# A two-problem cached decode attention on one core: q for two groups into four PSUM banks, wo as 512 + 64 columns of one weight load, and the output blocks folded on GpSimd before they are gathered

## Chip, core and metric

One core of one Trainium2 chip. The metric is device microseconds of one launch; a kernel's time is the median of its runs. A core has five engines that run their own instruction streams: TensorE (PE, with its weight loads PEld), VectorE (DVE), ScalarE (ACT), GpSimd (POOL) and SyncE (SP, which here only issues DMAs). Sixteen DMA engines move the data from HBM.

## What is computed

Two independent decode steps A and B with the same shapes; their outputs are laid side by side. The reference, cut to one of them:

```python
B, Sq, D = 2, 1, 576
Hq, Hkv, Sk, Dh = 32, 16, 16384, 128
W = min(4096, max(256, Sk // 4))        # 4096
rep = Hq // Hkv                         # 2
q = (x @ wq).reshape(B, Sq, Hq, Dh).transpose(0, 2, 1, 3)
k = jnp.repeat(k_cache[:, :, Sk - W:, :], rep, axis=1)
v = jnp.repeat(v_cache[:, :, Sk - W:, :], rep, axis=1)
scores = jnp.einsum("bhqd,bhkd->bhqk", q, k) * (Dh ** -0.5)
p = _softmax(scores, axis=-1)
o = jnp.einsum("bhqk,bhkd->bhqd", p, v)
return o.transpose(0, 2, 1, 3).reshape(B, Sq, Hq * Dh) @ wo
```

One query token per batch row, 32 query heads on 16 key heads, a window of the last 4096 keys, all in bfloat16. Nearly all bytes are the K and V windows: 2 problems x 2 batches x 16 heads x 4096 x 128 elements for each.

## The kernel before

**Steps and slabs.** The work is cut into 16 steps (ND = 16), eight for A and eight for B. Step s takes the keys of key heads s and s + 8 of both batch rows: one K slab and one V slab of 4 MB each (a partition row of 32 KB). Two steps make a group G = s // 2 (NG = 8); four groups make a problem. Slabs go through a ring of four buffers (`ring`, NR = 4). SP issues the loads in the order of `stream`: wq of A, wq of B, then K and V alternately, V one step behind K; at the end the order is K13, V12, K14, K15, V13, V14, V15. A slab's load waits until the last reader of the slab four places earlier is done (`issue_slab`, L228). V15 is loaded in two pieces of 3 MB and 1 MB with a semaphore each. The rows of wo that a group needs (`wob`, 1.15 MB) are loaded between slabs; those of the last group come at the very end, as one load of 576 KB and three small ones for its last four heads (L281, L266).

**The front.** x of both problems is loaded first and transposed; `do_qproj` (L394) makes q for one group in two PSUM banks (`tb0`, `tb1`), five matmuls of 512 columns each, ACT copies both to `qrow`, DVE transposes (`qtr`), ACT rearranges (`qk`). `init_mask` (L375) makes the mask tile `maskB` with four matmuls and one ACT copy.

**A step.** DVE transposes the K slab in four quarters (`do_X`, L459, buffers `xt`), PE multiplies each quarter with the spread q (`do_S`, eight matmuls of 512 columns over L482 and L166) into the scores bank pair `st0` or `st1`. One step later DVE takes the maximum, PE and DVE turn it into a bias (`do_nm`, `do_nm2`, `do_exp`), ACT does the exponential with its row sums (L527), DVE transposes the result (`do_pC`, L535), POOL spreads the row sums (`do_sum`, L543: `rsel`), PE sums them over the partitions once per group (`do_tot`, L547), and PE multiplies with the V slab (`do_PV`, L574): 32 matmuls of 512 columns, of which four run side by side in four strips of 32 columns of the array, into the bank `acc`. So PV of step c runs at the end of step c + 1 of the loop.

**A group's end.** `acc` holds, in each strip, four blocks of 128 columns of which one is wanted per row. ACT copies it to `acc_sb` (L586); `do_comb` gathers the wanted blocks with four small matmuls per step against `ident_r` (L603) into the bank `ot`, which DVE has set to zero; DVE multiplies with the reciprocal row sums and spreads the result (`do_norm`, L619, L630); `do_redist` turns it with two small matmuls (L661) and ACT copies it (`Rsb`, L669). `do_proj` (L676) then multiplies with wo: for each of eight heads of a batch row two matmuls of 288 columns, with a weight load each, that write to two different strips (partitions 0 and 32 of `ot`):

```python
return OT[32 * half:32 * half + Bb, ACC0:ACC0 + NH]
...
for half in range(2):
    last = e.matmul(proj_out(half), l_, wob[:, pc, s_, half * NH:(half + 1) * NH],
```

**The end.** Every engine's order is the order in which the program adds its instructions; nothing is reordered later. After the loop of steps the order is written out by hand: PV of step 13 in parts between the steps of the last softmax, `tot7`, comb13, norm13, redist6, proj13, PV14, comb14, norm14, the first piece of PV15, redist7, the second piece, comb15, norm15, proj14, proj15, and two copies (`do_E`, one on DVE and one on ACT) and the output DMAs. "PV13" in this text is the V part of step 13, "comb13" its gathering, and so on.

Of the kernel before, what the change touches and what calls it, by code (L numbers as in the profile page):

```python
# [59 lines left out]
def build_kernel(nc, probs, out, cfg=None):  # L60
# [32 lines left out]
    ACC0 = 128  # L93
    assert NOUT % 2 == 0 and ACC0 + NH <= 512
# [11 lines left out]
    with es:  # L106
# [32 lines left out]
        mrow = sb("mrow", [4, 128], BF16)  # L139
        mcol = sb("mcol", [4, 512], BF16)  # L140
# [3 lines left out]
        acc_sb = sb("acc_sb", [128, 512], BF16)  # L144
        ident_r = sb("ident_r", [128, 32], BF16)
        out_sb = sb("out_sb", [34, NPROB, NH], BF16)
# [33 lines left out]
        def load_x(P, eng):  # L180
# [7 lines left out]
        p_zxT = S.add("pool", lambda e: e.memset(xT[:].rearrange("c h p w -> c (h p w)").bitcast(FP32), 0.0), [], "zero_xT")  # L188
        p_zq = S.add("pool", lambda e: e.memset(zq[:].rearrange("d p z w -> d (p z w)").bitcast(FP32), 0.0), [], "zero_zq")
        p_ones_f = S.add("pool", lambda e: e.memset(ones_f[:], 1.0), [], "ones_f")  # L190
        p_ident_f = S.add("pool", lambda e: e.affine_select(ident_f[:], ones_f[:], [[-1, 128]], ALU.is_equal, 0.0,
                                                           base=0, channel_multiplier=1), [p_ones_f], "ident_f")
        p_zc = S.add("pool", lambda e: e.memset(mcol[:], 0.0), [], "zero_mcol")
        p_mcol = S.add("pool", lambda e: e.affine_select(
            mcol[:].rearrange("k (j c) -> k j c", c=4), mcol[:].rearrange("k (j c) -> k j c", c=4),
            [[0, 128], [1, 4]], ALU.is_equal, BIG, base=0, channel_multiplier=-1), [p_zc], "mcol")
        p_mrow = S.add("pool", lambda e: e.affine_select(
            mrow[:].rearrange("k (x c r) -> k x c r", c=4, r=2), ones_b[0:4, :].rearrange("k (x c r) -> k x c r", c=4, r=2),
            [[0, 16], [1, 4], [0, 2]], ALU.is_equal, 0.0, base=0, channel_multiplier=-1), [p_ones_b], "mrow")
# [95 lines left out]
        comb_bank = []  # L295
        q_first = [None, None]
        tb_consumer = {}
# [9 lines left out]
        ot_zero = {}  # L307
        ot_da = {}
        ot_pe = {0: None}
        acc_zero = {}  # L310
# [7 lines left out]
        def tb_job(fn, tag, deps):  # L318
            n = tbn[0]
            tbn[0] += 1  # L320
            bank = TB[n % NTB]
            d = list(deps)
            if n >= NTB:
                d.append(tb_consumer[n - NTB])
            return n, bank, S.add("pe", lambda e: fn(e, bank), d, tag)

        def init_small():
            ot_zero[0] = S.add("dve", lambda e: e.memset(OT[:], 0.0), [], "zero_OT")
            ot_da[0] = ot_zero[0]
            acc_zero[0] = ot_zero[0]  # L330
# [9 lines left out]
                mask4S[:], ident_b[:].rearrange("d (a s) -> d s a", s=4), AX.X, ALU.max), [p_ident_b], "mask4S")  # L340
            init["ident_r"] = S.add("dve", lambda e: e.tensor_reduce(
# [33 lines left out]
        def init_mask():  # L375
            def f(e):
                last = None
                for n_ in range(4):
                    bank = ST[1 - n_ // 2][:, 512 * (n_ % 2):512 * (n_ % 2) + 512]
                    if n_ == 0:  # L380
                        first = last = e.matmul(bank, mrow[:, :], mcol[:, :], start=True, stop=True)
                    else:
                        last = matmul_again(e, first, bank, mcol[:, :], True, True)
                return last
            op = S.add("pe", f, [p_mcol, p_mrow], "maskp")
            init["maskB"] = S.add("act", lambda e: e.activation(maskB[:], ST[1][:, 0:512], ACTF.Copy), [op], "maskB")
            chain[(0, "fill")] = chain[(1, "fill")] = init["maskB"]

        def do_fill(s):
            chain[(s, "fill")] = S.add("act", lambda e: e.activation(  # L390
                ST[s % 2][:, :].rearrange("k (h j) -> k h j", h=2), maskB[:].unsqueeze(1).broadcast_to([128, 2, 512]), ACTF.Copy),
                [init["maskB"], chain[(s - 2, "exp")], chain[(s - 2, "max")], zqev[s]], "fill%d" % s)

        def do_qproj(G):  # L394
            P = G // GPP
            nq = pos[("Q", P)]
            issue_until(nq)
            evs = []
            for nb in range(2):
                hf = nb  # L400
                c0 = nb * HH + 512 * (G % GPP)

                def fn(e, bank, c0=c0, hf=hf, nb=nb):
                    last = None
                    chs = list(range(NFC - 1)) + [NFC, NFC - 1]
                    for k_, ch in enumerate(chs if nb == 0 else chs[::-1]):
                        w_ = ring[:, nq % NR, ch * HD + c0:ch * HD + c0 + 512] if ch < NFC else wqr[:, P, c0 - hf * HH:c0 - hf * HH + 512]
                        x_ = xT[:, ch if ch < NFC else NFC + hf, P, :]
                        if k_ == 0 and q_first[0] == (P, ch):
                            last = matmul_again(e, q_first[1], bank[:, 0:512], w_, True, False, False)  # L410
                        else:
                            last = q_first[1] = e.matmul(bank[:, 0:512], x_, w_, start=(k_ == 0), stop=(k_ == NFC))  # L412
                        q_first[0] = (P, ch)
# [479 lines left out]
```

## Time and profile before

| what | value |
|---|---|
| median of 3 runs | 364.8 us (364.79 to 364.89) |
| the profiled execution: its time | 364.83 us |
| the profiled execution: its span, first to last instruction | 363.2 us |
| DMA | 153.27 MB in 7075 packets, mean 422 GB/s over the span |
| PE, PEld, DVE, ACT, POOL busy | 61%, 18%, 55%, 19%, 5% of the span |
| mean granted PE clock | 0.836 |
| PE instructions in the profile | 1370 matmuls, 1097 weight loads |

The span is what the engines did; some 1.6 us of the execution's time lie outside it. In the page, a row reads: source line, engine, operation, what it writes and reads, shapes, count, then busy time and mean duration of one, then the idle time before it and what ended that. PEclk is the clock that the throttle granted to PE (1.00 or 0.50 over a stretch), DMA share the mean busy share of the sixteen DMA engines.

### The profile page before, as it was taken

The numbers are of one execution on the slowest core, as the hardware profiler recorded it, in microseconds if no ns is written. First come the engines' busy times: TensorE is split into PE (matmuls) and PEld (weight loads), VectorE is DVE, ScalarE is ACT, GpSimd is POOL, SyncE is SP. The second block draws the span as 40 slices with busy tenths as digits, with TensorE's granted clock in tenths as the row PEclk, the third lists the DMA queues.
The fourth block names the chain that finished last, engine by engine and source line by source line (L and its number), as shares of the span: only waits on it lengthen the run. The fifth ranks groups of instructions, "written<-read, shape, count | busy, mean of one in ns | idle before, by whom it ended". The sixth has DMA issues, their size and how long they took to land.

```text
span 363.2 us, 2960 instructions
## 1 busy us (share of the span) xinstructions
PE 220.4 (61%) x1370; PEld 64.6 (18%) x1097; DVE 198.7 (55%) x173; ACT 67.8 (19%) x155; POOL 16.4 (5%) x45
## 2 busy tenths in 40 slices
PE   0399688292836748093754839184673918377875
PEld 0033112020211212021211202021120202111131
DVE  2022796573908476382916658191935649099821
ACT  1046203020300303020300303020020203002121
POOL 5000000000000000000000000000000000000000
PEclk9999899698895969678895958879696978858988
DMA  8999999999999999999999999999999999999994
GB/s 347 433 433 433 433 402 463 415 451 413 423 444 419 444 417 437 437 420 444 416 441 429 433 433 422 431 429 437 407 446 437 426 437 437 420 433 426 431 412 187
DMA packets 7075, 153.27 MB, mean 422 GB/s; under 512 B 780, under 2 KB 1304, under 8 KB 1688
## 3 DMA queue, kind: packets, MB, share of 16 engines
q1 hardware_dynamic: 7056, 153.10, 98.4%
q8 instruction: 9, 0.15, 0.2%
q10 hardware_dynamic: 8, 0.00, 0.0%
q14 instruction: 2, 0.02, 0.0%
HBM read 153.10 MB, written 0.00 MB: 422 GB/s over the span
## 4 chain that ended last, share of the span: by engine, by line
DMA 70%; DVE 14%; PE 12%; ACT 2%; issue 0%; SPq 0%; DVEq 0%
DMA ring<-in_B_k_cache_dram 34%; DMA ring<-in_A_k_cache_dram 25%; DVE xt L459 13%; DMA ring<-in_B_v_cache_dram 8%; PE st L482 4%; PE st L166 4%; DMA x_sb<-in_B_x_dram 3%; PE tb L412 3%; ACT qrow L421 1%; PE tb L166 1%; DVE qtr L427 1%; DVE nM L505 1%; ACT qk L435 0%; PE ot L689 0%; PE tb L495 0%
## 5 line engine op out<-in xcount | busy, mean ns | idle before, releaser
L459 DVE STREAM_TRANSPOSE xt<-ring 128x2048 f32<-128x2048 f32 x64 | 144.9, 2285 | 107.6 <-DMA ring<-in_B_k_cache_dram 59.5
L482 PE MATMUL st<-xt,zq 128*128 128x512 bf16 x256 | 114.6, 448 | 119.9 <-DVE xt L459 119.9
L166 PE MATMUL st<-xt,zq 128*128 128x512 bf16 x256 | 113.0, 441 | 0.0
L482 PEld LDWEIGHTS st<-xt,zq 128*128 128x128 bf16 x256 | 27.5, 107 | 209.2 <-DVE xt L459 136.5
L510 ACT ACTIVATE nMrep<-nM 1x128 f32<-1x128 f32 x16 | 4.9, 308 | 176.8 <-DVE nM L505 176.8
L574 PE MATMUL acc<-ring,pC 128*32 128x512 bf16 x512 | 32.8, 391 | 1.3 <-DMA ring<-in_B_v_cache_dram 1.2
L535 DVE STREAM_TRANSPOSE pC<-pR 128x1024 bf16<-128x1024 bf16 x16 | 19.4, 1214 | 4.3 <-ACT pR L527 2.1
L586 ACT ACTIVATE acc_sb<-acc 128x512 bf16<-128x512 f32 x16 | 9.5, 597 | 63.2 <-PE acc L574 63.2
L492 DVE TENSOR_REDUCE m<-st 128x1 f32<-128x1024 f32 x16 | 19.0, 1190 | 1.0 <-PE st L166 0.9
L527 ACT ACTIVATE pR<-st,bias_sb 128x1024 bf16<-128x1024 f32 x16 | 17.8, 1114 | 0.5
L412 PE MATMUL tb<-ring,xT 128*128 128x512 bf16 x50 | 16.7, 424 | 0.1
L427 DVE STREAM_TRANSPOSE qtr<-qrow 128x512 f32<-128x512 f32 x8 | 5.7, 711 | 19.4 <-ACT qrow L421 19.4
L574 PEld LDWEIGHTS acc<-ring,pC 128*32 128x32 bf16 x512 | 13.1, 98 | 17.1 <-issue 6.0
L543 POOL TENSOR_SCALAR rsel<-maskS,rsum 128x8 f32<-128x8 bf16 x16 | 4.9, 308 | 243.8 <-ACT pR L527 243.8
L390 ACT ACTIVATE st<-maskB 128x1024 f32<-128x1024 bf16 x14 | 14.4, 1028 | 0.4
L446 POOL TENSOR_TENSOR zq<-qk,maskA 128x128 bf16<-128x128 bf16 x16 | 6.4, 400 | 86.7 <-PE st L166 69.6
L421 ACT ACTIVATE qrow<-tb 128x512 bf16<-128x512 f32 x16 | 9.3, 586 | 3.8 <-PE tb L412 3.6
L689 PE MATMUL ot<-wob,Rsb 128*2 128x288 bf16 x120 | 9.5, 303 | 0.3 <-ACT Rsb L669 0.3
L353 PE MATMUL tb<-ident_b,x_sb 4*128 4x4 bf16 x4 | 0.3, 172 | 14.6 <-DVE x_dup L360 14.6
L412 PEld LDWEIGHTS tb<-ring,xT 128*128 128x128 bf16 x50 | 5.2, 106 | 11.7 <-issue 7.8
L412 PE MATMUL tb<-wqr,xT 128*128 128x512 bf16 x16 | 6.7, 417 | 0.0
L505 DVE TENSOR_REDUCE nM<-tb 1x8 f32<-1x128 f32 x16 | 4.4, 273 | 4.1 <-PE tb L495 4.1
(64 smaller groups left out, 79.0 us busy)
## 6 DMA issues: line engine op xcount, KB each, us to landing
ring<-in_A_k_cache_dram SPq DMA_DIRECT2D x8, 4096.0 KB, 30.6
ring<-in_A_v_cache_dram SPq DMA_DIRECT2D x8, 4096.0 KB, 35.4
ring<-in_B_k_cache_dram SPq DMA_DIRECT2D x8, 4096.0 KB, 30.7
ring<-in_B_v_cache_dram SPq DMA_DIRECT2D x7, 4096.0 KB, 35.2
wob<-in_A_wo_dram SPq DMA_DIRECT2D x4, 1152.0 KB, 37.1
ring<-in_A_wq_dram SPq DMA_DIRECT2D x1, 4096.0 KB, 12.7
ring<-in_B_wq_dram SPq DMA_DIRECT2D x1, 4096.0 KB, 21.7
wob<-in_B_wo_dram SPq DMA_DIRECT2D x3, 1152.0 KB, 37.4
```

Of the source, the lines that this page charges most:

```text
L166: return e.add_instruction(mybir.InstMatmult(name=nc.get_next_instruction_name(), engine=i.engine, ins=[e.lower_ap(rhs), i.ins[1]], outs=[ ...
L390: chain[(s, "fill")] = S.add("act", lambda e: e.activation(ST[s % 2][:, :].rearrange("k (h j) -> k h j", h=2), maskB[:].unsqueeze(1).broad ...
L412: last = q_first[1] = e.matmul(bank[:, 0:512], x_, w_, start=(k_ == 0), stop=(k_ == NFC))
L421: evs.append(S.add("act", lambda e, bank=bank, nb=nb: e.activation(qrow[:, 512 * nb:512 * nb + 512], bank[:, 0:512], ACTF.Copy), d, "qrow% ...
L459: Xop[(s, u)] = S.add("dve", lambda e: e.transpose(xt[:, i % NKT, :].rearrange("k (j w) -> k j w", w=64), ring[:, n % NR, :].bitcast(FP32) ...
L482: first = last = e.matmul(bank, zq[:, p4, s % NZQ, w0:w0 + 128], mv, start=False, stop=stop, skip_group_check=True)
L492: chain[(s, "max")] = S.add("dve", lambda e: e.tensor_reduce(m1[:, 0:1], ST[s % 2][:, :], AX.X, ALU.max), d, "max%d" % s)
L527: chain[(s, "exp")] = S.add("act", lambda e: e.activation(pR[:, :], ST[s % 2][:, :], ACTF.Exp, bias=bias_sb[:, 0:1], scale=SCALE, accum_ou ...
L535: chain[(s, "pC")] = S.add("dve", lambda e: e.transpose(pC[:, s % NPT, :, :].rearrange("k j c -> k (j c)"), pR[:, :]), d, "pC%d" % s)
L574: last = e.matmul(ACC[32 * cb:32 * cb + 32, 0:512], pC[:, D_ % NPT, j0_:j0_ + 4, :].rearrange("k j c -> k (j c)"), ring[:, n % NR, j0_ * 1 ...
L586: acc_ev[D_] = S.add("act", lambda e: e.activation(acc_sb[:], ACC[:, :], ACTF.Copy), d, "accev%d" % D_)
L689: last = e.matmul(proj_out(half), l_, wob[:, pc, s_, half * NH:(half + 1) * NH], start=False, stop=True, skip_group_check=True)
```

## The change

PE's instruction list gets 46 matmuls, 143 weight loads and 9 waits shorter, 198 in all:

- **q:** `do_qpair` makes q for two groups at once, in four banks, and runs the four banks one after the other on each loaded x. The 80 matmuls stay; 66 weight loads become 22. `qrow` copies go with it (1024 columns at once for every second pair).
- **mask:** `maskB` is made by two DVE instructions instead of four matmuls and an ACT copy. Three memsets go from POOL to DVE, three POOL instructions go away.
- **fold:** after the ACT copy of `acc`, POOL multiplies with a 0/1 mask and adds the four blocks in two halvings (`accm`, `acca`, `accr`; both steps of a group in one instruction each, in group 6 each step by itself), and `do_comb` needs one small matmul per step. Groups 0 to 6 do so; steps 14 and 15 are gathered as before. `ot` needs no zeroing any more.
- **wo:** for groups 0 to 6 each head is one weight load with a matmul of 512 columns and one of 64 columns. The 512 columns add up in `ot` over a problem's groups, the 64 columns go to a `tb` bank and DVE adds them up in `o_rest`. Before the last two steps, `fin_ops` puts both into the two-strip form, and proj14 and proj15 add to it as before.
- **row sums:** one `rsel` per group (POOL, now a tensor-tensor) instead of two, added to POOL's list in `do_tot`.
- **order in a step:** the last quarter of the scores, `do_S(s, 3)`, waits for pC of the step before (not in the last step); a group's proj comes after it; comb, norm and redist move one quarter later.
- **order at the end:** PV14 comes before comb13; comb13, comb14, redist6 and proj13 come between PV14 and the first piece of PV15. On POOL, the three folding instructions of step 13 stand ahead of `rsel7`.
- **output:** three output DMAs instead of four.

```diff
-        p_zxT = S.add("pool", lambda e: e.memset(xT[:]...
+        p_zxT = S.add("dve", lambda e: e.memset(xT[:]...
...
+        def do_qpair(i):
+            Gs = (2 * i, 2 * i + 1)
...
+            order = [NFC, NFC + 1] + list(range(NFC))
+            if Gs[0] % GPP:
+                order = order[::-1]
+            todo_ = [(ch, b) for ch in order for b in mine(ch)]
...
+                        if q_first[0] == (P, ch):
+                            last = matmul_again(e, q_first[1], banks[b], w_, start, stop, False)
...
         def do_S(s, u):
...
+            if u == NU - 1 and 1 <= s < ND - 1:
+                deps.append(chain[(s - 1, "pC")])
...
-        def do_sum(s):
...
         def do_tot(G):
+            d = [chain[(2 * G, "exp")], chain[(2 * G + 1, "exp")], init["maskS"]]
+            if G >= 1:
+                d.append(chain[(G - 1, "tot")])
+            chain[(G, "rsel")] = S.add("pool", lambda e: e.tensor_tensor(
+                rsel[:, :, :], maskS[:].unsqueeze(1).broadcast_to([128, 2, 8]),
+                rsum[:].unsqueeze(2).broadcast_to([128, 2, 8]), ALU.mult), d, "rsel%d" % G)
...
         def do_PV(D_, rounds, wait):
...
+                acc_ev[D_] = S.add("act", lambda e: e.activation(acc_sb[:, D_ % 2, :], ACC[:, :], ACTF.Copy), d, "accev%d" % D_)
+                G = D_ // 2
+                if not by_group(G) or (D_ % 2 == 0 and G < NG - 2):
+                    return
+                l0, l1 = (0, 2) if G < NG - 2 else (D_ % 2, D_ % 2 + 1)
...
+                t = S.add("pool", lambda e: e.tensor_tensor(
+                    v, v, maskJ[:].unsqueeze(1).unsqueeze(3).broadcast_to([128, l1 - l0, 4, 128]), ALU.mult),
+                    [acc_ev[2 * G + l] for l in range(l0, l1)] + [init["maskJ"]], "accm%d" % D_)
+                t = S.add("pool", lambda e: e.tensor_tensor(a_[:, :, 0:256], a_[:, :, 0:256], a_[:, :, 256:512], ALU.add),
+                          [t], "acca%d" % D_)
...
+                t = S.add("pool", lambda e: e.tensor_tensor(
+                    acc_r[:, l0:l1, :], a_[:, :, 0:128], a_[:, :, 128:256], ALU.add), d, "accr%d" % D_)
...
         def do_comb(D_):
...
+                    for l_ in range(2):
+                        last = e.matmul(bank[:, 8 * l_:8 * l_ + 8], acc_r[:, l_, :], maskS[:, :], start=True, stop=True)
...
         def do_proj(D_):
...
+                        if by_group(G):
+                            first = e.matmul(OT[0:Bb, 0:NB0], l_, wob[:, pc, s_, 0:NB0], start=start and begin, stop=end, skip_group_check=True)
+                            last = matmul_again(e, first, rest[0:Bb, 0:NB1], wob[:, pc, s_, NB0:NOUT], rstart and begin, rstop and end)
...
+                    elif G == NG - 2:
+                        d = [proj[D_], chain[(ND - 2, "exp")], chain[(ND - 2, "max")]]
+                        a_ = S.add("act", lambda e: e.activation(fin(0), OT[0:Bb, 0:NH], ACTF.Copy), d, "fin0")
+                        tb_consumer[n] = S.add("dve", lambda e: e.tensor_tensor(
+                            fin(1)[:, NB0 - NH:NH], o_rest[:, :], bank[0:Bb, 0:NB1], ALU.add), d + [rest_add[G - 1]], "fin1")
+                        fin_ops.append(S.add("dve", lambda e: e.tensor_copy(fin(1)[:, 0:NB0 - NH], OT[0:Bb, NH:NB0]), [a_], "fin2"))
...
         do_PV(D_, range(4, NRD), None)
-        do_sum(s)
         do_tot(s // 2)
+        do_rsb(s // 2)
+        do_PV(ND - 2, range(NRD), None)
         do_comb(D_)
         do_norm(D_)
-        do_rsb(s // 2)
+        do_comb(ND - 2)
         do_redist(D_ // 2)
+        do_norm(ND - 2)
         do_proj(D_)
-        do_PV(ND - 2, range(NRD), None)
-        do_comb(ND - 2)
-        do_norm(ND - 2)
         D_ = ND - 1
```

## Prediction

> **What bounds the kernel now.** First the slices and queues of the page, then the DMA issues.
>
> ```profile
> DMA  8999999999999999999999999999999999999994
> ...
> q8 instruction: 9, 0.15, 0.2%
> ...
> ring<-in_A_k_cache_dram SPq DMA_DIRECT2D x8, 4096.0 KB, 30.6
> ...
> ring<-in_B_v_cache_dram SPq DMA_DIRECT2D x7, 4096.0 KB, 35.2
> ```
>
> The DMA engines never rest between the first slice and the last. A 4 MB slab (4.19 million bytes) takes 9.7 us at the 433 GB/s of most slices; a K slab lands 30.6 us after its issue, a V slab 35.2, so each issue has 21 and 25 us of other transfers ahead of it. Work that delays an issue by less costs nothing. What counts is the end of the stream and what follows the last pieces of V and wo. So next the timeline of the end (start, duration):
>
> ```profile
> 347.48 0.31 POOL L543 TENSOR_SCALAR rsel<-maskS,rsum 128x8 f32<-128x8 bf16 x1 [7.02 <-ACT pR L527]
> 347.85 0.40 PE L547 MATMUL tb<-rsel,ones_f 128*128 128x16 f32 x2 [0.92 <-POOL rsel L543]
> ...
> 350.79 0.61 PE L574 MATMUL acc<-ring,pC 128*32 128x512 bf16 x2
> ...
> 355.61 1.48 PE L574 MATMUL acc<-ring,pC 128*32 128x512 bf16 x24 [0.29 <-DMA ring<-in_B_v_cache_dram]
> ...
> 358.10 0.62 PE L574 MATMUL acc<-ring,pC 128*32 128x512 bf16 x8 [0.88 <-DMA ring<-in_B_v_cache_dram]
> ...
> 359.60 0.66 PE L689 MATMUL ot<-wob,Rsb 128*2 128x288 bf16 x8
> ...
> 360.30 1.12 PE L689 MATMUL ot<-wob,oTn 128*2 128x288 bf16 x8
> ```
>
> PV15's pieces start as they land (355.6, 358.1); proj15 ends on the last rows of wo, whose load ends its chain at 360.95. The two copies end at 361.91; a span of 363.2 and a time of 364.83 follow, 0.03 above the median of 364.8. I sum against 361.91.
>
> Last, PE's clock in stretches of 3.41 us, cut where it changes (PE busy is the second number, granted clock the third from last):
>
> ```profile
> 111.07:114.48 3.41, 2.56 (x7) 0.54 (x4) 3.41 (x3) 0.00 (x0) 0.00 (x0) 0.50 0.94 403
> 172.51:175.92 3.41, 2.65 (x7) 0.54 (x4) 3.41 (x3) 0.00 (x0) 0.00 (x0) 0.50 1.00 432
> 346.59:350.00 3.41, 1.23 (x20) 0.69 (x14) 1.94 (x6) 1.48 (x4) 0.31 (x1) 1.00 0.94 401
> 350.00:353.42 3.41, 3.41 (x40) 2.14 (x39) 0.00 (x0) 0.00 (x0) 0.00 (x0) 0.50 0.96 406
> 353.42:356.83 3.41, 2.41 (x43) 0.98 (x34) 0.59 (x2) 0.60 (x1) 0.00 (x0) 1.00 0.98 395
> 356.83:360.24 3.41, 1.83 (x30) 0.67 (x22) 0.17 (x1) 0.78 (x2) 0.00 (x0) 1.00 0.50 182
> ```
>
> A stretch's work sets the next one's clock: 1.23 and 1.83 us of mixed work at full clock are followed by half clock. At half clock 2.65 us bring full clock back in the next stretch, 2.56 do not. At half clock a matmul of 512 columns takes 0.43 us, at full clock 0.216 (spacing of starts).
>
> **The change part by part.**
>
> *Front.* The four mask matmuls (14.94 to 16.67) go, so q starts about 1.6 us sooner; 44 weight loads go too, but 80 matmuls of 0.216 to 0.43 us cover them. Gain 0: q releases V0 (issued at 28.73) and K2 (38.31), each with over 14 us of loads ahead. Three memsets that DVE takes over (some 1.5 us on POOL) lie in its wait for x until 14.25; without that cover they would delay q, which is itself hidden.
>
> *Steps 0 to 13.* S(s,3) now waits for pC, behind the last transpose on DVE: up to 1.25 us. Queued behind it on PE are the group's proj and PV of the step before, and SP's next V load waits for that PV. proj of a group grows: its two 288-column halves run side by side in two strips, 16 in 1.15 us at full clock; 512 and 64 columns of one load share a strip, 8 x (0.216 + 0.027) = 1.95 us, 3.9 at half clock. Together under 4 us, inside the 25 us; the DVE idles 107.6 us in all before K transposes, 6.7 a step. POOL's folds of 1024, 512 and 256 columns cost at most 6 us per group of 41. The matmuls and loads that go from comb lie in that slack. All 0.
>
> *The fold at the end.* This is on the path. acc of step 13 is copied by 347.88 (ACT, 347.29 + 0.59). Then POOL folds 512, 256 and 128 columns, and only behind them comes `rsel7`, which before ran at 347.48. PE's list is `tot7`, PV14, so PV14, whose slab has long landed, waits too. No fold is in the trace. Bounds from POOL's rows: rsel (0.308 us for 8 columns) and zq (0.400 for 128) give 0.77 ns a column, so 0.70 + 0.50 + 0.40 = 1.6; zq taken as all per column gives 1.6 + 0.8 + 0.4 = 2.8. I take 2.1, nearer the line, as zq is the same operation but rsel is not. With 0.31 for rsel7 and four hand-overs of 0.09 (exp's end at 347.39 to rsel at 347.48), rsel7 ends at 350.65; tot7 to the next PE work is 0.24 plus a hop, so PV14 starts at 350.95 (350.45 to 351.65). Before: 350.79, but with comb13, redist6 and proj13 already done, which now stand behind it.
>
> The Trainium skill (GPSIMD Engine Reference, 3.1) gives 4497 ns for a two-input add of 2048 fp32 columns, an estimate of 1.97 us for the three, and its 4.1 sends elementwise work to VectorE; by it PV14 would start at 350.8.
>
> *PE behind it.* PE has nothing from 346.97 to 350.6, more than a stretch, so PV14 starts at half clock: 8 rounds x 0.43 = 3.4, to 354.4. ACT's copy to 355.2, comb14 to 355.5, redist6 to 355.75, Rsb to 356.0. In the stretch from 350.00 to 353.42 PE works 2.5 us at half clock, under the 2.56 that did not bring it back. If it stays half, proj13 is 8 x 0.48 = 3.84 us; it works without a gap, so the clock returns at the first boundary with 2.6 us of it behind, 358.6 at the earliest: proj13 ends at 359.2 (359.85 for the boundary at 360.24). PV15's first piece, landed, 1.3 us: 360.5; redist7 and second piece 0.9: 361.4; copy 0.6 and hops, comb15 0.3: 362.4; proj14 and proj15 1.15 at full clock: 363.5; copies 0.45 and a hop: 364.0. Against 361.91: 2.0 us late (2.9 with the later boundary). The last wo rows have landed. fin0 to fin2 (three small copies, 0.45 us each) run beside PV15 and are due at proj14, more than 2 us later. I take 2.0.
>
> *Instruction loads.* q8 fetches PE's instructions, nine packets of 16 KB. Read packet by packet, each holds one of the sixteen DMA engines 1.0 to 1.1 us and slows its next packet by 0.47. Each transfer ends in sixteen completion marks: those of V14 spread over 2.16 us, and after the ninth fetch (349.92) one share of V15 is 1.12 us behind all others: by the marks, the share that the first fetch (46.15) had already set back. It sets the landings at 355.6, 358.1 and 360.95; in the last microsecond one engine alone still moves wo. From the ninth fetch to the end PE issued 204 instructions; the change takes out 198. So the ninth fetch falls off the end of the stream, and last V and wo land 1.1 us sooner. In the forecast that gains 0, since PV15 and proj15 wait for proj13. The Trainium skill (Runtime: NRT & Kernel Launch, Instruction fetch mechanics) states blocks of 16 KiB, 256 instructions, and calls the crossing mostly hidden; here it delays a share.
>
> *Rest.* The last copies stay side by side (0.40 and 0.45); output A is issued long before: 0.
>
> **Sum:** 364.83 + 2.0 = 366.8.
>
> **The rivals.**
>
> *The clock comes back in time.* The same late PV14, but the boundary lies so that 2.6 us of work precede it, or the fold is at its low bound. Then PV14 ends near 354.0, proj13 runs 355.5 to 357.5, PV15 to 359.5, copies at 361.9 to 362.5: 364.8 to 365.4, middle 365.1. For it: 2.5 against 2.6 is a hair. Against: the idle PE before PV14. The Trainium skill (TensorE: Matmul & The Clock Gate, Part 1) calls the 3.41 us window free-running; the rows' spacing agrees, and by it executions could differ in which case they fall into; one trace can't show that.
>
> *Faster: the lost fetch is paid out.* The last landings come 1.1 us sooner and PE is ready for them: 364.83 - 1.1 = 363.7, in part 364.1. It decides where proj13 ends before 355.6 (357.0 less the first piece's 1.5). Counting back at full clock (1.95 + 0.8 + 0.85 + 1.9) PV14 must start by about 350.1, at half clock for PV14 by 348.5: folds of 1.2 us or less together, below my bound. For it: POOL's fixed part may overlap from one instruction to the next. Against: PE's cold start.
>
> *Dearer folds.* Above 2.8 us, for the shared mask operand's sake: PV14 after 351.7, all later by the same, 368.2 or more.
>
> **How the numbers follow.** Forecast (clock stays low) 0.48, clock back 0.27, faster 0.17, dearer 0.08. 0.2% (0.73 us) is what a measurement of this kernel tells from no change: faster is below 364.07, slower above 365.53. The clock-back case gives 0.24 to no change and 0.03 to slower; so faster 0.17, same 0.24, slower 0.59. The forecast's own range is 366.3 to 367.8 (fold bounds and the boundary's place); the whole range reaches to the other cases: 363.9 to 367.8.
>
> **What would show it.** Right: `rsel` of the last group behind three POOL instructions that end near 350.3; PV14 near 351; granted clock 0.50 while the 512-column proj matmuls run; PV15's first piece starting on PE's own order, not on a DMA; eight q8 packets before the last V piece instead of nine. Wrong: PV15 still waiting for DMA, PV14 before 350.1, or the ninth packet still near 350. A different landing of K15 or V14 would upset the sum at its root.

## The result, and the profile after the change

| kernel | median, us | runs (from to) | ratio to the kernel before, 95% interval |
|---|---|---|---|
| before | 364.86 | 18 (364.53 to 365.63) | 1 |
| changed | 365.4 | 18 (364.98 to 367.33) | 1.0025 [1.0013, 1.0036] |
| changed, second set | 365.38 | 11 (364.46 to 366.48) | 1.0014 [1.0004, 1.0024] |
| changed, third set | 366.19 | 8 (364.50 to 366.77) | 1.0027 [1.0014, 1.0040] |

The change makes the kernel a little slower: 0.5 us in the first set, where 2.0 were forecast. In that set its times spread over 2.35 us, those of before over 1.1. The first profile is of an execution of 366.16 us, among the longer ones. This is its timeline at the end (start, duration, engine, line, operation, idle time before it and what ended that):

```profile
346.44 0.59 ACT L613 ACTIVATE acc_sb<-acc 128x512 bf16<-128x512 f32 x1
...
347.10 1.04 POOL L620 TENSOR_TENSOR acc_sb<-acc_sb,maskJ 128x512 bf16<-128x512 bf16 x1 [18.91 <-ACT acc_sb L613]
348.21 0.67 POOL L623 TENSOR_TENSOR acc_sb<-acc_sb 128x256 bf16<-128x256 bf16 x1
348.96 0.42 POOL L628 TENSOR_TENSOR acc_r<-acc_sb 128x128 bf16<-128x128 bf16 x1
349.34 0.22 POOL L572 TENSOR_TENSOR rsel<-maskS,rsum 128x16 f32<-128x16 bf16 x1
...
349.61 0.61 PE L575 MATMUL tb<-rsel,ones_f 128*128 128x16 f32 x2 [3.55 <-POOL rsel L572]
...
350.15 3.60 PE L601 MATMUL acc<-ring,pC 128*32 128x512 bf16 x32
...
355.18 0.59 PE L734 MATMUL ot<-wob,Rsb 128*2 128x512 bf16 x1 [0.27 <-ACT Rsb L707]
...
355.64 0.61 PE L734 MATMUL ot<-wob,Rsb 128*2 128x512 bf16 x1
...
356.12 0.61 PE L734 MATMUL ot<-wob,Rsb 128*2 128x512 bf16 x1
...
358.04 0.61 PE L601 MATMUL acc<-ring,pC 128*32 128x512 bf16 x3
...
360.31 0.61 PE L601 MATMUL acc<-ring,pC 128*32 128x512 bf16 x8
...
363.01 0.40 ACT L770 ACTIVATE out_sb<-st 2x288 bf16<-2x288 f32 x1 [1.43 <-PE st L738]
```

The three folds (L620, L623, L628) stand ahead of `rsel7` (L572), and PE's 3.55 us of idle time end with it. PV14 starts at 350.15 and runs for 3.60 us, half speed; proj13's heads follow each other at 0.48 us, half speed too; both pieces of PV15 start with no DMA behind them, in PE's own order. This is the forecast chain, link by link. The copies end at 363.46; before they ended at 361.91.

The page's row for the instruction queue, and two of the rows of DMA issues (KB each, us to landing):

```profile
q8 instruction: 8, 0.13, 0.1%
...
ring<-in_A_v_cache_dram SPq DMA_DIRECT2D x8, 4096.0 KB, 32.4
...
ring<-in_B_v_cache_dram SPq DMA_DIRECT2D x7, 4096.0 KB, 32.6
```

Eight fetches instead of nine lie in the span, and the last completion mark of wo is at 359.8 where it was at 360.5. V is issued some 2.6 us later than before (35.2 then) and, less the 9.7 us of its own slab, still has nearly 23 us of other transfers ahead.

Why then 365.4? Stretches of 3.41 us in three profiles of the same changed kernel (PE busy is the second number, granted clock the third from last). The first profile, time 366.16:

```profile
348.35:351.76 3.41, 2.15 (x18) 1.11 (x22) 0.26 (x1) 0.00 (x0) 1.13 (x3) 0.50 1.04 447
351.76:355.17 3.41, 2.59 (x28) 0.92 (x20) 1.03 (x5) 0.78 (x2) 0.00 (x0) 0.50 0.88 371
355.17:358.58 3.41, 3.40 (x21) 1.02 (x14) 0.22 (x1) 0.00 (x0) 0.00 (x0) 0.50 0.94 364
358.58:361.99 3.41, 2.71 (x46) 1.07 (x38) 0.68 (x3) 1.14 (x3) 0.00 (x0) 1.00 0.16 56
```

The second, time 365.02:

```profile
353.84:357.25 3.41, 3.14 (x18) 0.93 (x11) 0.64 (x3) 0.18 (x1) 0.00 (x0) 0.50 1.00 402
357.25:360.67 3.42, 2.71 (x42) 1.04 (x38) 0.61 (x2) 1.14 (x3) 0.00 (x0) 0.99 0.38 136
```

And the third, span 363.0:

```profile
349.69:353.10 3.41, 3.16 (x30) 1.50 (x34) 0.26 (x1) 0.00 (x0) 0.20 (x2) 0.50 0.99 423
353.10:356.52 3.42, 2.58 (x32) 0.97 (x19) 1.25 (x5) 0.78 (x2) 0.00 (x0) 1.00 0.92 378
```

Full clock returns at 358.6, 357.3 and 353.1, which are no whole number of stretches apart: where the boundaries lie differs between executions of one program. In the first, all of proj13 runs at half clock; in the second, six of its eight heads; in the third, none, though PV14 is as late (350.48). The Trainium skill (TensorE: Matmul & The Clock Gate, Part 1) calls the 3.41 us window free-running; the three profiles agree.

The place of the boundaries moves the start of PV14 as well. In step 14 the clock is low too, and the chain that ended last runs there from K14's landing over the scores' matmuls and DVE's work to exp15 (the exponential of step 15). The table has the four profiles of the changed kernel, in us:

| profile | K14 lands | clock back in step 14 | exp15 starts | PV14 starts | clock back behind PV14 | copies end | span |
|---|---|---|---|---|---|---|---|
| second | 318.0 | 323.2 | 344.58 | 349.40 | 357.3 | 362.45 | 363.8 |
| first | 318.3 | 324.5 | 345.33 | 350.15 | 358.6 | 363.46 | 364.8 |
| fourth (third set) | 318.1 | 325.1 | 345.42 | 350.24 | 359.3 | 363.85 | 365.2 |
| third | 317.9 | 325.8 | 345.66 | 350.48 | 353.1 | 361.70 | 363.0 |

The later the clock comes back in step 14, the later exp15 and PV14 start: counted from K14's landing, 26.6 us where it comes back after 5.2 us, 27.7 where it comes back after 7.9. The other profiles of this case, of other kernels, lie in the same order. In the first three rows the clock stays low behind PV14 until proj13 is nearly or quite done; in the last it comes back 2.6 us after PV14's start. That one place of the boundaries sets both is read from the profiles; no run here sets it.

All 38 executions of the changed kernel fall by their spans into 7 of 363.0 to 363.4, 18 of 363.8 to 364.5 and 13 of 364.8 to 365.6, and a set's median depends on how many of each it has. The third profile is of the shortest group, the second of the middle one, the first and fourth of the longest. So by its one profile the middle group has the low clock too, only earlier.

### The profile page after: what moved, and what is told of

The parts are those of the page before. It is cut to its first block, busy times and chain, and to the rows that moved or that the text cites. A ratio compares the mean times of both kernels' runs of the same rounds, so it can differ in the third digit from the quotient of the medians.

```text
span 364.8 us, 2762 instructions
## 1 busy us (share of the span) xinstructions
PE 229.9 (63%) x1323; PEld 59.6 (16%) x954; DVE 201.5 (55%) x176; ACT 68.7 (19%) x153; POOL 35.2 (10%) x55
## 4 chain that ended last, share of the span: by engine, by line
DMA 63%; DVE 17%; PE 17%; ACT 1%; POOL 1%; issue 1%; SPq 0%; DVEq 0%
DMA ring<-in_B_k_cache_dram 34%; DMA ring<-in_A_k_cache_dram 26%; DVE xt L487 15%; PE st L169 6%; PE st L512 4%; DMA x_sb<-in_B_x_dram 3%; PE acc L601 2%; PE st L423 1%; PE ot L734 1%; PE tb L169 1%; DVE nM L535 1%; DVE m L522 1%; PE ot L169 1%; PE tb L423 1%; PE acc L169 1%
## 5 line engine op out<-in xcount | busy, mean ns | idle before, releaser
L512 PE MATMUL st<-xt,zq 128*128 128x512 bf16 x256 | 116.2, 454 | 112.3 <-DVE xt L487 85.9
L169 PE MATMUL st<-xt,zq 128*128 128x512 bf16 x256 | 114.8, 448 | 0.0
L601 PE MATMUL acc<-ring,pC 128*32 128x512 bf16 x512 | 37.4, 408 | 0.0
L620 POOL TENSOR_TENSOR acc_sb<-acc_sb,maskJ 128x1024 bf16<-128x1024 bf16 (+1 forms) x8 | 13.4, 1679 | 79.3 <-ACT acc_sb L613 79.3
L734 PE MATMUL ot<-wob,Rsb 128*2 128x512 bf16 x56 | 18.0, 439 | 0.3 <-ACT Rsb L707 0.3
L388 ACT ACTIVATE st<-maskB 128x1024 f32<-128x1024 bf16 x16 | 16.5, 1031 | 1.6 <-POOL rsel L572 0.4
L572 POOL TENSOR_TENSOR rsel<-maskS,rsum 128x16 f32<-128x16 bf16 x8 | 1.7, 216 | 106.9 <-ACT pR L557 106.9
L169 PE MATMUL tb<-wob,Rsb 128*2 128x64 bf16 x56 | 11.7, 209 | 0.0
L623 POOL TENSOR_TENSOR acc_sb<-acc_sb 128x512 bf16<-128x512 bf16 (+1 forms) x8 | 8.2, 1030 | 0.6
L734 PEld LDWEIGHTS ot<-wob,Rsb 128*2 128x2 bf16 x56 | 5.3, 95 | 16.0 <-issue 14.4
```

Of the source, the lines that this page charges most:

```text
L169: return e.add_instruction(mybir.InstMatmult(name=nc.get_next_instruction_name(), engine=i.engine, ins=[e.lower_ap(rhs), i.ins[1]], outs=[ ...
L388: chain[(s, "fill")] = S.add("act", lambda e: e.activation(ST[s % 2][:, :].rearrange("k (h j) -> k h j", h=2), maskB[:].unsqueeze(1).broad ...
L512: first = last = e.matmul(bank, zq[:, p4, s % NZQ, w0:w0 + 128], mv, start=False, stop=stop, skip_group_check=True)
L601: last = e.matmul(ACC[32 * cb:32 * cb + 32, 0:512], pC[:, D_ % NPT, j0_:j0_ + 4, :].rearrange("k j c -> k (j c)"), ring[:, n % NR, j0_ * 1 ...
L620: t = S.add("pool", lambda e: e.tensor_tensor(v, v, maskJ[:].unsqueeze(1).unsqueeze(3).broadcast_to([128, l1 - l0, 4, 128]), ALU.mult), [a ...
L623: t = S.add("pool", lambda e: e.tensor_tensor(a_[:, :, 0:256], a_[:, :, 0:256], a_[:, :, 256:512], ALU.add), [t], "acca%d" % D_)
```

## The experiments

**The changed kernel again**, for more profiles (read above):

> The changed kernel once more, unchanged, for a second profile and more times: its 18 times stand in two groups, ten at 364.98 to 365.41 and eight at 366.03 to 367.33, and the profile at hand is of the second. Theory (the 3.41 us stretches of the clock lie differently in each execution): where the profile is of the first group, the folds are as long (2.1 us) and PV14 starts as late (near 350.2), but the clock is back before or early in proj13, which takes 2.0 to 2.8 us instead of 3.8, and the boundaries of the clock do not lie at 348.4 and 358.6 modulo 3.413. Rival (the groups come from the DMA stream, whose start differed by up to 0.6 us between profiles): folds, PV14 and clock as in the first profile relative to the stream, and the last marks of wo 0.5 us or more earlier.

> The changed kernel a third time, for one more profile: same theories and numbers as for the second.

The theory held in the main: folds of 2.13 us in both, and the clock's boundaries elsewhere. But PV14 started at 349.40 and 350.48, not at 350.2 in both, and 0.75 of the 1.01 us by which the second profile's copies end before the first's are there when PV14 starts. The rival fell: the last mark of wo was at 359.4 in both, 0.4 sooner than in the first profile, but the end waited for PE and not for it.

**rsel7 first.** `do_rsel` is the POOL instruction that stood in `do_tot`.

```diff
+        do_rsel(s // 2)
         do_PV(D_, range(4, NRD), None)
         do_tot(s // 2)
```

> The changed kernel with rsel7 put on POOL ahead of the three folds of step 13; nothing else moves. Theory (POOL's order is what delays PV14, and behind it proj13 and PV15): rsel7 at 345.5, tot7 at about 346.7, PV14 before 347.5 instead of 350.15, proj13 done by 354.5 even at half clock, PV15's pieces and proj15 wait for DMA again. Last marks of wo stay near 359.6 (360.52 before), so the copies end near 361.0 and the time is 363.6 to 364.1 in nearly all runs, 0.8 to 1.2 below the kernel before. Rival (the wider proj at half clock alone costs it): proj13 still ends after 356 and the time stays at 365.0 to 366.2.

Measured: 364.14 (12 runs, 363.08 to 364.87), ratio 0.9973 [0.9960, 0.9987]. `rsel7` itself starts at 346.63, behind the exponential, and not at 345.5. Its timeline:

```profile
346.63 0.21 POOL L572 TENSOR_TENSOR rsel<-maskS,rsum 128x16 f32<-128x16 bf16 x1 [18.32 <-ACT pR L557]
...
347.12 1.04 POOL L624 TENSOR_TENSOR acc_sb<-acc_sb,maskJ 128x512 bf16<-128x512 bf16 x1 [0.27 <-ACT acc_sb L617]
...
347.46 1.91 PE L605 MATMUL acc<-ring,pC 128*32 128x512 bf16 x32 [0.16 <-DMA ring<-in_B_v_cache_dram]
...
354.76 1.48 PE L605 MATMUL acc<-ring,pC 128*32 128x512 bf16 x24 [1.69 <-DMA ring<-in_B_v_cache_dram]
...
357.25 0.62 PE L605 MATMUL acc<-ring,pC 128*32 128x512 bf16 x8 [0.88 <-DMA ring<-in_B_v_cache_dram]
```

PV14 is back at 347.46, at full clock, and both pieces of PV15 wait for DMA again. The place of the cost is shown: three POOL instructions ahead of `rsel7`. "Nearly all runs" was wrong: seven spans at 361.8 to 362.5, five at 363.1 to 363.5.

**proj13 in two strips**, the late `rsel7` kept (the edit is shown in part; a new `do_fin` makes the two-strip form ahead of proj13).

```diff
-                parts = [([(Rsb[:, pc, :, s_], s_) for s_ in range(8)], [r_ev[G]], new, True, True)]
+                parts = [([(Rsb[:, pc, :, s_], s_) for s_ in range(8)], [r_ev[G]] + fin_ops, False, False, False)]
```

> The changed kernel with proj13 as two strips of 288 columns (as before the change), by putting the sums of groups 4 and 5 into the two-strip form before proj13 instead of after; rsel7 stays behind the folds. Theory (PV14 late by POOL, then PE work at half clock adds up): PV14 still at about 350.2, proj13 2.0 us instead of 3.8 at half clock, copies end near 361.7 where the clock is low and near 361.0 (last landings) where it is back: 363.8 to 364.8. Rival (the late PV14 alone is the cost, the width of proj is hidden): 365.0 to 366.2 as the changed kernel.

Measured: 365.04 (364.49 to 366.25), ratio 1.0005 [0.9993, 1.0017]. proj13 took 2.0 us instead of 3.8 (355.04 to 357.1), as expected, but PV15 still stood behind it, and the time is 0.2 above the theory's range, at the low end of the rival's. That is 0.4 below the changed kernel, whose own sets differ by 0.8, so by the medians the share of proj's width is not told apart from the clock's place. The profile says more: with the clock back at 358.1, 12.15 us lie between PV14's start (350.00) and the end of the copies, where the changed kernel's three profiles with low clock have 13.05 to 13.61. So the width seems to cost about a microsecond there; one profile does not show it.

**PE kept warm**, first with the ninth fetch in the way, then without it.

```diff
+        S.add("pe", lambda e: [e.matmul(ST[s % 2][...], pC[...], ring[...], start=True, stop=True) for k in range(12)][-1], ...)
         do_tot(s // 2)
```

> The changed kernel with 12 matmuls of 512 columns that nobody reads (into the scores bank of step 15, done by then) on PE ahead of tot7; the wait for POOL stays. Theory (the wait of 2.6 us is paid for by the clock that falls in it, not by the wait itself): PV14 still starts near 350.2 but runs at full clock in 1.9 us instead of 3.6, proj13 ends near 355.5, copies near 361.0 to 361.5, time 363.7 to 364.5 and no run above 365. Rival (the wait itself is the cost): 365.0 to 366.2, PV15 still behind proj13.

Measured: 364.70 (364.49 to 364.97), ratio 0.9996 [0.9987, 1.0004], 0.2 above the range. The end of its timeline:

```profile
349.90 1.91 PE L601 MATMUL acc<-ring,pC 128*32 128x512 bf16 x32
...
360.79 0.93 PE L738 MATMUL st<-wob,oTn 128*2 128x288 bf16 x8 [1.47 <-DMA wob<-in_B_wo_dram]
```

PV14 is as late as in the changed kernel, yet runs at full clock in 1.91 us; what ends the kernel is no longer PE but the last rows of wo, and these are late: the added instructions had brought the ninth fetch to 358.17, and one share of wo's marks trailed the rest by 1.35 us (360.97 against 359.62). So the same with 63 PE instructions left out early (part of the products with wo is then missing):

```diff
+                parts = [([... for s_ in range(1 if G in (0, 1, 4) else 8)], ...)]
```

> The changed kernel with the 12 matmuls that nobody reads ahead of tot7, and proj of groups 0, 1 and 4 cut to one head of eight (63 PE instructions fewer; that part of the products with wo is left out). The warm kernel before had its ninth fetch at 358.17 and one share of wo 1.1 us behind. Theory (clock and fetch are the two prices, the wait itself costs nothing): no ninth fetch, last mark of wo near 359.7, copies end near 361.0, times 363.0 to 363.9. Rival (the wait costs by itself): 364.4 to 365.0 as with the ninth fetch.

Measured: 363.42 (6 runs: four at 363.21 to 363.45, two at 364.07 and 364.37), ratio 0.9967 [0.9955, 0.9979]. The ninth fetch was not gone but came at 360.11, behind the last mark of wo (359.4). The spans are all 361.8 to 362.1, as with `rsel7` first and the same 63 left out (below), while PV14 starts at 350.37. The wait for POOL by itself costs nothing in the span; the half clock that it leaves behind does.

**The ninth fetch put back, and taken away.** rsel7 first, with 198 tiny matmuls at the start of PE's list:

```diff
+        S.add("pe", pad, [p_ones_b], "pad")
         init_mask()
```

> The kernel with rsel7 first, and 198 tiny matmuls (8 columns, one weight load, result read by nobody) at the start of PE's list, where PE waits for x: as many PE instructions as the kernel before has. Theory (the ninth instruction fetch sets one DMA share back by 1.1 us): nine q8 packets of PE's instructions, the ninth between 346 and 351, one share of V15 behind the others by about 1 us, last mark of wo 0.8 to 1.2 later than with rsel7 first alone, time 0.7 to 1.2 longer than it, so 364.4 to 365.2. Rival (fetches are hidden; the stream sets its end by itself): within 0.2 of rsel7 first.

Measured: 364.49 (364.24 to 365.46), ratio 0.9992 [0.9983, 1.0001]. The ninth fetch was back, at 347.20, and the last mark of wo at 360.55 instead of 359.70, though the slabs stood 0.3 us earlier. The lowest time rose by 1.16, the median by only 0.35 where 0.7 to 1.2 were expected, since six runs of rsel7 first are long themselves. Two more kernels asked why. One filled PE's wait ahead of PV15 with matmuls that nobody reads:

```diff
+        S.add("pe", lambda e: [e.matmul(ST[s % 2][...], ...) for k in range(8)][-1], ...)
         do_PV(D_, range(PIECES[0][0] // JR, PIECES[0][1] // JR), pieces[0])
```

> The kernel with rsel7 first, and 8 matmuls of 512 columns that nobody reads on PE between proj13 and the first piece of PV15, where it waits for DMA from 352.9 to 354.8. The times of rsel7 first stand in two groups, 363.1 to 363.8 and 364.5 to 364.9. Theory (the upper group is PE at half clock in PV15 and proj15): the clock stays up, nearly all runs 363.0 to 363.9. Rival (the upper group comes from elsewhere, such as a fetch that sets the last rows of wo back): both groups stay and the median is 363.9 to 364.4.

Measured: 363.80 (9 runs), ratio 0.9973 [0.9962, 0.9983]. The median lies in the theory's range, but the upper group of spans did not go: two of nine stand at 363.1 and 363.6 (five of twelve with `rsel7` first alone). A third long run, of 364.47, has a short span (362.2) and 2.27 us outside it. So the clock is not all of the upper group; nine runs do not show whether it has a part. The other kernel left the 63 PE instructions out:

> The kernel with rsel7 first, and proj of groups 0, 1 and 4 cut to one head of eight: 63 PE instructions fewer, early, where PE has slack; that part of the products with wo is left out. In rsel7 first the ninth fetch lay at 359.39, just ahead of the last marks of wo, and its runs stand in two groups (spans 361.8 to 362.5, and 363.1 to 363.5). Theory (the upper group is the ninth fetch that takes hold of a DMA engine before the last rows of wo): with the ninth fetch gone the upper group goes; spans 361.6 to 362.6, times 362.9 to 363.9, and no run above 364.2. Rival (the upper group is PE at half clock in the tail): two groups as before, median 363.8 to 364.4.

Measured: 363.16, all five runs at 363.06 to 363.27, ratio 0.9951 [0.9938, 0.9963]. The spans are all 361.8 to 362.0: the upper group is gone, as the theory of the fetch had it. Last, the kernel before without its ninth fetch:

```diff
-                parts = [([(Rsb[:, pc, :, s_], s_) for s_ in range(8 if by_group(G) else 4)], ...
+                parts = [([(Rsb[:, pc, :, s_], s_) for s_ in range((1 if G < 6 else 8) if by_group(G) else 4)], ...
...
-                    for j4 in range(4):
+                    for j4 in range(1 if D_ < 12 else 4):
...
-                for jr in rounds:
+                for jr in ((0, last_r) if D_ == 0 else rounds):
```

> The kernel before the change with 288 PE instructions left out early, in PE's slack: proj of groups 0 to 5 one head of eight, comb of steps 0 to 11 one block of four, PV of step 0 two rounds of eight; those parts of the result are left out. Everything from step 12 on is as before. Theory (the ninth fetch, at 349.92 before, sets the last rows of V and wo back by 1.1 us): eight q8 packets, last mark of wo near 359.5 instead of 360.5, copies end about 1 us sooner, time 363.6 to 364.1. Rival (the fetch is hidden): 364.6 to 365.0.

Measured: 363.60 (363.36 to 363.93), ratio 0.9964 [0.9951, 0.9976]: 1.4 below its own runs of before (364.98). The last copies, in its timeline:

```profile
356.88 0.61 PE L574 MATMUL acc<-ring,pC 128*32 128x512 bf16 x8 [0.88 <-DMA ring<-in_B_v_cache_dram]
...
360.44 0.40 ACT L698 ACTIVATE out_sb<-ot 2x288 bf16<-2x288 f32 x1 [2.29 <-PE ot L689]
```

The second piece of PV15 starts at 356.88 (before 358.10), released by its DMA, and the copies end at 360.89 (before 361.91). Nothing from step 12 on was edited. So the ninth 16 KB fetch costs the kernel before 1.0 us up to the last copies and, by the ratio, 1.3 of time. Its late place alone is not what costs: the trimmed kernel has its eighth and last fetch at 348.20. There the last two of the sixteen marks of V15's first piece lie 0.06 us apart (354.29 and 354.35), while in the kernel before the ninth fetch leaves one share 1.1 us behind all others (355.56 against 354.45). With `rsel7` first and the ninth fetch put back at 347.20, one share is 1.27 us behind. The Trainium skill (Runtime: NRT & Kernel Launch, Instruction fetch mechanics) calls such a crossing mostly hidden; here the ninth is not.

**The changed kernel without a ninth fetch**, the same 63 PE instructions of the products with wo left out:

> The changed kernel with the same 63 PE instructions of proj of groups 0, 1 and 4 left out and nothing else, so that no ninth fetch can come before the end. Theory (in the changed kernel the end waits for PE, so the ninth fetch costs only where it lies after the last instruction): spans as the changed kernel's, 363.0 to 365.6, time outside the span 1.2 to 1.4 in nearly all runs, median 364.9 to 365.5. Rival (the fetch also sets the landings that count there): spans about a microsecond shorter, median 364.4 or less.

Measured: 365.31 (12 runs, 364.33 to 366.73), ratio 1.0010 [0.9996, 1.0023]; spans 363.0 to 365.5, and 1.22 to 1.33 outside in every run. With the late `rsel7` the lost fetch gains nothing, as the theory had it: the end waits for PE.

**Without the wait of S(s,3) for pC.**

```diff
-            if u == NU - 1 and 1 <= s < ND - 1:
-                deps.append(chain[(s - 1, "pC")])
```

> The changed kernel without the wait of the last quarter of the scores for pC of the step before. Theory (that wait lies in slack, as the prediction had it): the same within 0.3 of 365.4. Rival (the wait moves matmuls so that step 15 ends sooner, by the clock): exp15 0.5 to 0.9 later, PV14 at 350.7 or later, time 365.9 or more.

Measured: 366.80 (5 runs, 366.24 to 367.57), ratio 1.0050 [1.0037, 1.0062]. It looked as if the wait were worth 1.4 us. Its stretches behind PV14's start at 350.52:

```profile
349.52:352.93 3.41, 2.95 (x26) 1.42 (x30) 0.26 (x1) 0.00 (x0) 0.41 (x2) 0.50 0.93 396
352.93:356.35 3.42, 2.59 (x23) 0.81 (x14) 1.26 (x5) 0.78 (x2) 0.00 (x0) 0.50 0.95 394
```

PE was busy for 2.95 us in a stretch and stayed at half clock; the third profile of the changed kernel had 3.16, with the boundary 0.17 later, and came back. exp15 began at 345.70, next to the changed kernel's 345.66, so the rival's later step 15 is not in this profile. Three further kernels, and the changed kernel beside the last of them, asked whether wait or clock made the difference:

> The kernel with rsel7 first and 63 PE instructions of proj of groups 0, 1 and 4 left out (that part of the products with wo is missing), now also without the wait of the last quarter of the scores for pC. Without that wait the changed kernel took 366.8 instead of 365.4. Theory A (the wait acts only through the clock in which the late PV14 and proj13 run): with rsel7 first PV14 is early and the end waits for DMA, so 363.0 to 363.5, as the same kernel with the wait (363.16). Theory B (the wait also lets the softmax of step 15 or the stream end sooner): 363.7 to 364.5.

> The changed kernel without the wait for pC once more, for a second profile. Theory A (the clock in the tail): exp15 between 344.5 and 345.8 as in the changed kernel's profiles, PV14 and all eight heads of proj13 at half clock. Theory B (step 15 late): exp15 at 346.0 or later.

> The changed kernel without the wait for pC a third time, beside the changed kernel on the same chip. Theory (the five runs at 366.2 to 367.6 all had the clock stretches lie badly, and the wait itself is worth little): runs in both groups, below 365.4 and above 366, and a median within 0.5 of the changed kernel's. Rival (the wait is worth more than a microsecond): median 366.3 or more, with the changed kernel at 365.0 to 365.6.

> The changed kernel beside its version without the wait for pC, on the same chip: 365.0 to 365.6 by all theories, in two or three groups by the place of the clock stretches.

Measured: with rsel7 first and no wait, spans of 361.8 to 362.2, as with the wait (361.8 to 362.0); the median of 363.51 (ratio 0.9966 [0.9953, 0.9978]) is above 363.16 by two runs with 2.06 and 2.44 outside the span.

The single run took 364.89, with proj13 at full clock. Its exp15 began at 346.14, which is the sign of theory B and not of A. But the table above accounts for it without the wait: the clock came back in step 14 at 326.3, later than in its four rows, and the next boundaries (350.2, 353.6) brought it back behind PV14 with 3.19 us of work.

On one chip, without the wait 365.65 (12 runs, 364.21 to 367.32, ratio 1.0014 [0.9998, 1.0029]), with it 366.19, above the 365.0 to 365.6 expected by all theories. So the wait gains nothing that this set can measure. Why all five spans of the first set were long (365.0 to 366.3) stays open: of the twelve here three are, and five in a row would then be rare, so the place of the clock need not be drawn afresh for each run of a set. That set had no runs of the changed kernel on the same chip beside it. A median of five runs was no measurement here.

**A version that beats both**, with nothing left out: rsel7 first, `rsel` in bfloat16, and the 64 last columns of a group's heads as one matmul.

```diff
-        rsel = sb("rsel", [128, 2, 8], FP32)
+        rsel = sb("rsel", [128, 2, 8], BF16)
...
-                            last = matmul_again(e, first, rest[0:Bb, 0:NB1], wob[:, pc, s_, NB0:NOUT], rstart and begin, rstop and end)
+                            if end:
+                                last = e.matmul(OT[32:32 + 8 * Bb, 0:8 * NB1], Rsb[:, pc, :, :].rearrange("d b s -> d (b s)"),
+                                                wob[:, pc, :, NB0:NOUT], start=start, stop=True, skip_group_check=True)
```

> A version that computes everything: rsel7 first; rsel in bfloat16 so that tot is one matmul instead of two; and the 64 last columns of wo of a group's eight heads as one matmul of 16 rows by 512 columns (all head pairs, the wanted ones picked by a mask once per problem) instead of eight of 64. About 55 PE instructions fewer than the changed kernel, nothing left out. Theory (late PV14 and the ninth fetch are the two prices): the ninth fetch is gone or comes after the last rows of wo; last marks of wo near 359.6, copies end near 360.7, times 363.0 to 363.7 and none between 364.4 and 365.0. Rival (the ninth fetch only moves to the end and lengthens the time there by about a microsecond, or proj13's extra hand-overs delay PV15): 363.9 to 364.6.

Measured: 363.50 (6 runs, 363.17 to 363.75), ratio 0.9948 [0.9932, 0.9964]. Its timeline:

```profile
347.12 1.91 PE L606 MATMUL acc<-ring,pC 128*32 128x512 bf16 x32 [0.47 <-DMA ring<-in_B_v_cache_dram]
...
351.38 0.38 PE L741 MATMUL ot<-wob,Rsb 128*16 128x512 bf16 x1
...
354.42 1.48 PE L606 MATMUL acc<-ring,pC 128*32 128x512 bf16 x24 [0.86 <-DMA ring<-in_B_v_cache_dram]
...
360.13 0.40 ACT L782 ACTIVATE out_sb<-st 2x288 bf16<-2x288 f32 x1 [1.96 <-PE st L745]
```

PV15 waits for DMA, no ninth fetch lies in the span, and the copies end at 360.58, 1.3 before those of the kernel before.

## Why the prediction was right or wrong

- **Front, and steps 0 to 13 at 0: right, as far as shown.** V is still nearly 23 us ahead of its need; the pC wait is worth nothing measurable in a joint set.
- **The fold: right.** 2.13 us (1.04, 0.67, 0.42) against 2.1.
- **The clock behind it: right in kind.** If the middle group is as its one profile, it stays low in 31 of 38 executions; the forecast gave that 0.48. From PV14's start to the end of the copies the sum has 13.05 us (364.0 less 350.95); the three profiles with low clock have 13.05, 13.31 and 13.61.
- **The step that failed is the start of PV14, "so PV14 starts at 350.95", and with it the boundaries of the clock: both were taken from one execution of before.** Measured starts are 349.40, 350.15, 350.24 and 350.48. The folds are as long as forecast, but the softmax of step 15 ends sooner: exp15 starts at 344.58 to 345.66, where the profile of before has 346.19. In that profile the clock came back in step 14 at 326.1, later than in any row of the table, and was low once more from 332.9 to 336.4. The kernel before without its ninth fetch, with the clock back at 324.4, has 344.94, so the earlier start goes with the clock and needs no help from the change. In the second profile the start is 1.55 us ahead of the forecast; with the 0.4 less outside its span that makes up the 1.8 us between 366.8 and its 365.02.
- **Where the low clock was right, the reason was partly luck.** "In the stretch from 350.00 to 353.42 PE works 2.5 us at half clock, under the 2.56" does not hold where the boundaries lie nearly so: in the third profile (349.7 to 353.1) PE works 3.16 us and the clock comes back, and the span is the shortest of the four. The 2.5 counts PV14 alone and leaves out `tot7`, which has 0.24 us in the sum and takes 0.54 at half clock ahead of PV14. The clock stayed low where the boundaries lay otherwise.
- **The threshold was mis-sized as well.** In the profile of before 2.56 us did not and 2.65 did bring the clock back; in this tail 2.95 and, in the changed kernel without a ninth fetch, 3.04 did not, while 3.14, 3.16 and 3.19 did.
- **The rival "clock comes back in time" (365.1) was nearer to the median by luck.** Its case is that of the seven shortest spans, and the median lies in the middle group.
- **What lies around the span: missed.** 1.55 to 1.68 us in the runs of before beside the experiments, 1.21 to 1.40 in 30 of 38 of the changed kernel. The sum kept 1.63; the 0.3 went unforeseen.
- **Instruction loads: right.** The last marks of wo came 0.7 to 1.1 sooner (1.1 forecast) and gained 0 behind the late PE, as forecast. The ninth fetch came behind the last mark of wo in every profile: at 361.81, 364.35 and 363.05 in three, and not at all in the first.
- **The "faster" rival's price: right within 0.5.** 363.7 forecast for PE in time; 363.16 with rsel7 first and no ninth fetch, 363.60 for the kernel before without it.

In sum, the change has a gain of over a microsecond in it (fewer PE instructions, and so no ninth fetch in the stream). Three folds ahead of one small POOL instruction hold it back, by the clock that falls while PE waits, and 0.5 us of loss are left.

## What to carry to other kernels

Put the small instruction that PE waits for ahead of long ones on an in-order engine: at the end of this kernel that order alone was worth 1.3 us (365.4 to 364.14), and 2.1 where no ninth fetch came either (365.31 to 363.16). A wait on PE is to be priced with the clock that it takes down, and as a spread, since the place of the clock's stretches differs between executions; start times and boundaries read from one profile are one draw. Where DMA is the bound, count the instruction fetches that fall into the stream: dropping the ninth, which by the marks fell on a share already set back, was worth over a microsecond (364.98 to 363.60).

## What was unexpected in the hardware

- One kernel's spans spread over 2.6 us (363.0 to 365.6) and its sets' medians from 365.4 to 366.2. In four profiles, with spans of 363.0 to 365.2, this goes with the place of the clock's stretches, which sets both when step 15 ends and when the clock comes back.
- In 8 of 38 executions of the changed kernel 1.86 to 2.63 us lie outside the span instead of 1.21 to 1.40. The one such execution of it that was profiled (2.37) had its ninth fetch at 364.35, after the span's end at 363.0; another kernel's (2.27) at 363.47, after 362.2; where the fetch came before the last instructions it was 1.22 to 1.39. None of the 17 runs of the two kernels that keep the wait for pC and have 63 PE instructions fewer (`rsel7` first, and last) had it. But the version without that wait and with as many fewer had it twice in five, and one version that holds the clock up and has 63 fewer twice in six, so the fetch as its cause is likely, not shown.
- Why the changed kernel has 0.3 us less outside its span stays open. It isn't the number of PE instructions: 198 more left it at 1.22 to 1.31, and 288 fewer in the kernel before at 1.60 to 1.66.
